# A new instruction order, two more tiles transposed by DMA and two weight loads joined in an adaLN block with feature-map attention and a gated MLP

## The chip, the cores and the metric

The kernel runs on one core of one Trainium2 chip. The metric is the device time of one execution in microseconds (us): lower is better. The median of three runs is compared; beside it stands one execution that was recorded by the hardware profiler.

## The reference

One transformer block on 2048 tokens of width 512, in bfloat16. A modulation vector made from `c` gives a shift, a scale and a gate for the attention half and for the MLP half.

```python
mod = (silu(c) @ w_mod).reshape(1, 6, 1, 512)
sa, ca, ga, sb, cb, gb = (mod[:, i] for i in range(6))
h = layernorm(x) * (1 + ca) + sa
x = x + ga * A(h)
h = layernorm(x) * (1 + cb) + sb
x = x + gb * ((sigmoid(h @ w_gate) * (h @ w_up)) @ w_down)      # F = 1376

def A(h):                        # 32 heads of 16
    q, k, v = split(h @ wqkv)
    pq, pk = q @ w_phi, k @ w_phi                # per head
    phi_q = concat(softmax(pq), softmax(-pq))    # 32 features per head
    phi_k = concat(softmax(pk), softmax(-pk))
    kv = phi_k.T @ v;  z = phi_k.sum(over tokens)
    return ((phi_q @ kv) / (phi_q @ z + 1e-6)) @ wo
```

## The kernel before

**Tiles.** The 2048 tokens are 16 tiles of 128. All of x, the weights and the normalized, transposed input `h1T` stay in the core's memory (SBUF).

**Order.** Each piece of work is a small task with a name, an engine and a function. The text ORDER lists the names; each engine gets its instructions in this order and nothing is reordered later, so an engine whose next instruction waits holds back all that stands behind it on that engine. A suffix (@A ScalarE, @D VectorE, @P GpSimd) says which engine takes a task; without it the first engine in the task's table does. In the profile, TensorE is PE, VectorE is DVE, ScalarE is ACT, GpSimd is POOL, SyncE is SP. All loads, all stores and all transposes by DMA are issued by SP, in the order of the text too. Buffers of a class (eight PSUM banks, six `r2k` buffers and so on) are given out in the order of the text; the next user of a buffer waits for the last reader of the one before.

**Start.** `ld_...` tasks load x (`x0a` to `x3b`, two tiles each), the q, k, v weights (`wq`, `wk`, `wv`), the modulation weights (`wm..`), `wo`, the MLP weights (`wg`, `wu`, `wd`). `warm` tasks keep PE busy before there is real work. `tpw`, `wTc`, `fold`, `foldc` multiply w_phi into the k weights (side 1) and the q weights (side 0, where `wqT` transposes by DMA). `modc1`, `modca`, `modc2` make the modulation columns.

**First LayerNorm.** Tiles are taken in groups, LG: {0}, {1}, {2,3}, {4,5}, {6,7}, {8..11}, {12..15}. `st1_t` are the statistics of tile t (DVE), `rs1_g` and `nmr1_g` the factors of group g, `xn1_t` the normalized tile. Where TD of the group is 0, `tph` transposes by PE into PSUM and `hm1_gj` applies scale and shift from PSUM to column block j of `h1T`. Where TD is 1, `xT1_t` transposes by DMA straight into `h1T` and `hm1_gj` works there in place, SBUF to SBUF.

**Keys and values, per tile t.** `K` and `V` are four matmuls each; `e` (ACT) are the exponentials, `n` (DVE) their sums, `r` (DVE or ACT) the reciprocals, `phi` (POOL or DVE) the product of the two, `va` the copy of V, `kv` the matmuls that add phi.T @ v up in PSUM over all tiles. Tiles 11 to 15 are cut in parts (`e11.4` is the part that begins at column group 4). `kvm`, `kvp`, `kvz`, `kvn` turn the sum into the matrix for the queries.

```python
G.add(f"phi{t}.{a}", {"POOL": 0.08 + 1.77 * w, "DVE": 0.08 + 1.07 * w}, f_p, r=[("kr", t, a)], w=[("phi", t, a)], bufs=[ee, ks, ph], port=("POOL", "DVE"))
```

**Queries and output of the attention.** `Q` and `qe` are the query features of 512 tokens and 128 columns, `sm`, `num`, `den`, `u`, `o`, `oT`, `out` the quotient and the projection, `x1_t` the residual, `st2`, `rs2`, `nmr2`, `xn2`, `xnT`, `mod` the second LayerNorm of units of one or two tiles. `ga` and `gb` are written to memory and read back spread over all partitions (`gwa`, `gra`, `gwb`, `grb`) and multiplied into `wo` and `wd`.

**MLP.** It runs in chunks of 1, 1, 2, 4, 4, 4 tiles: `g` and `u` are the gate and up matmuls of a column tile, `tg` the tanh (ACT), `hm` the product (DVE), `y` the down projection, `fin` the residual sum (DVE), `st` the store. The last tile's y is cut into 384 and 128 columns (`y15.*` and `y15.*b`). `bnd` and `ldf` check a bound on the inputs and read a flag for a general path that the given inputs do not take.

Lines of the profile: 747 tpw, 751 wTc, 764 fold, 770 and 772 foldc, 787 and 788 st1, 803 nmr1, 812, 814 and 816 xn1 on ACT, DVE, POOL, 821 xT1, 829 tph, 836 and 838 hm1 on ACT and on DVE or POOL, 855 K, 859 V, 871 e, 874 n, 884 and 885 r on ACT, 887 r on DVE, 877 phi, 895 va, 278 kv, 299 kvm, 933 Q, 908 gra, 672 ld_wg, 663 ld_wv, 427 to 444 u, 562 to 567 g and u, 600 y, 607 fin, 609 st.

Of the kernel before, what the change touches and what calls it, by code (L numbers as in the profile page):

```python
# [38 lines left out]
st1_5 tph22 tph21 tph20 foldc13 rs1_3 warm1_11 foldc12 xn1_0 st1_6 st1_7 ld_wm01 warm1_12 modc1.0 foldc10 modc1.1 xn1_1@P ld_x2a ld_x2b rs1_4@P warm1_13
warm1_14 tph00 tph12 modc1c nmr1_3 xn1_5@P xn1_4@P tph13 warm1_15 tph23 hm1_21@A hm1_20 hm1_12 hm1_13 tph03 tph10 hm1_23 hm1_22@A hm1_10@A K3 nmr1_4 st1_10  # L40
tph01 tph02 tph11 hm1_11 hm1_00@A hm1_03@A hm1_01@A hm1_02@A ld_wq1 ld_wq0 ld_wv0 ld_wv1 K2 st1_11 st1_9 e3.0 K0 xn1_6@P xn1_7@P pmem e0.0 tph31 tph32 tph30
tph33 st1_8 n0.0 K1 hm1_30@A e1.0 hm1_31@A V3 tph42 V1 va3 r0.0@A rs1_5@P nmr1_5 hm1_32 hm1_33 ld_x3b ld_x3a wqT3 tph41 V4 hm1_41@A va1 K4 e2.0 xn1_8 n3.0
n1.0 ld_wmga xn1_11@P tph40 xn1_10@P xn1_9@P hm1_40 hm1_42 r1.0 K5 modca.0 modca.1 modcac phi0.0 st1_12 wqT0 wqT1 wqT2 fold01 r3.0@A xT1_11 xT1_10 phi1.0
fold00 tph43 foldc00 hm1_43@A fold03 xT1_9 foldc01 foldc03@D n2.0 V0 va0 e5.0 r2.0@A K6 V2 kv0.0 st1_13 st1_14 phi3.0 xT1_8 V6 kv1.0 e4.0 ld_wu0 phi2.0 K7 V5
st1_15 gwa va2 e6.0 rs1_6 va4 hm1_53@A va5 e7.0 fold02 kv2.0 kv3.0 V7 n4.0 hm1_51 hm1_50@P hm1_52@P n5.0 r4.0 phi4.0 nmr1_6 r5.0 phi5.0 xn1_12 ld_wd2 ld_wu1
ld_wg0 xT1_12 foldc02@D va6 xn1_14 xT1_14 K11 K8 V11 n6.0 va11@D n7.0 xn1_13@D kv4.0 K10 va7 r6.0@A e11.2 r7.0@A e8.0 phi6.0@D K9 xn1_15@D e11.4 e9.0 V10
kv5.0 n8.0 V8 phi7.0 va8 e11.0 r8.0 n9.0 e10.0 kv6.0 r9.0@A xT1_13 xT1_15 va10@D n11.4 V9 Q02 kv7.0 Q10 Q00 phi8.0 hm1_60 hm1_61 hm1_63 va9 hm1_62@A n10.0
r11.4 phi9.0 kv8.0 qe00 e11.6 K13 e13.4 r10.0 qe02 e13.0 K12 e12.0 n11.2 n13.4 n11.0 n11.6 r11.0 phi10.0 K15 phi11.0 n13.0 r11.6 r11.2 ld_wo r13.0 phi11.6
phi11.2 K14 V13 kv9.0 kv10.0 r13.4@A V12 n12.0 phi11.4@D e14.4 e15.0 V14 ld_wd va13 r12.0@A e15.4 phi13.0@D phi13.4 n15.0 n15.4 kv11.4 Q03 V15 e14.0 kv11.6
kv11.0 kv11.2 phi12.0 qe03 Q11 Q01 n14.4 n14.0 r14.4 r14.0 r15.0@A r15.4@A va12 va15 va14 qe01 Q13 kv12.0 kv13.4 phi14.4@D phi15.0@D phi14.0@D phi15.4@D  # L50
# [1071 lines left out]
```

## Time and profile before

| | us |
|---|---|
| median of 3 runs (213.63 to 215.25) | 213.74 |
| the profiled execution | 212.59 |
| its span | 210.9 |
| busy PE, DVE, ACT, POOL | 201.6, 168.4, 112.7, 92.6 |
| PE waiting for POOL's phi / DVE's h1T / DVE's u | 1.5 / 1.5 / 1.1 |
| first K matmul, kvm, first g matmul, last y | 12.9, 57.9, 74.1, 207.7 |

Times inside the span count from its start. An idle engine costs nothing unless something that sets the end waits for it; a wait is put down to the engine that released it. Busy PE counts overlapping matmuls once. PE's clock was granted in full throughout.

### The profile page before, as it was taken

What the parts mean: (1) busy time and instruction counts of PE and PEld (TensorE: products, weight loads), DVE (VectorE), ACT (ScalarE), POOL (GpSimd) and SP (SyncE); (2) the same over time, 40 slices, a digit from 0 to 9 for tenths busy, and PEclk for the clock granted to TensorE, in tenths of its full rate; (3) what the DMA queues carried; (4) which work ended last, traced back from release to release, by engine and by line L of the source; (5) the groups of instructions that cost most, each with busy time, mean ns of one, the idle gap of its engine ahead of it and who ended that gap; (6) DMA issues with size and microseconds to landing.
All of it is one profiled execution on the core that took longest, in us unless ns stands there. A gap on an engine that the chain in (4) does not pass through costs nothing.

```text
span 210.9 us, 4333 instructions
## 1 busy us (share of the span) xinstructions
PE 201.6 (96%) x1547; PEld 111.6 (53%) x1547; DVE 168.4 (80%) x425; ACT 112.7 (53%) x272; POOL 92.6 (44%) x118
## 2 busy tenths in 40 slices
PE   7999999959999999989999999999999999999993
PEld 2654655425676589748764444445444444444442
DVE  3899999999979998998999899874857756563522
ACT  2899999679998996445253322442251551323200
POOL 3667997558947599944243312515030210000000
PEclk9999999999999999999999999999999999999999
DMA  6999598398051110501623300325004030010111
GB/s 159 369 352 221 103 265 224 57 335 307 15 158 53 39 39 16 65 10 40 104 50 51 78 0 0 75 53 75 25 0 100 6 75 19 6 50 3 50 58 54
DMA packets 35309, 19.80 MB, mean 94 GB/s; under 512 B 23409, under 2 KB 34002, under 8 KB 35282
## 3 DMA queue, kind: packets, MB, share of 16 engines
q1 hardware_dynamic: 34752, 19.44, 36.1%
q8 instruction: 14, 0.23, 0.5%
q14 instruction: 13, 0.11, 0.2%
q10 hardware_dynamic: 530, 0.02, 0.1%
HBM read 12.11 MB, written 2.10 MB: 67 GB/s over the span
## 4 chain that ended last, share of the span: by engine, by line
PE 64%; DVE 16%; POOL 10%; DMA 4%; issue 3%; ACT 1%; SPq 0%; POOLq 0%; DVEq 0%; ACTq 0%
PE y_ps L600 15%; PE g_ps L562 14%; PE u_ps L562 14%; PE a_ps L471 4%; POOL phi L877 4%; PE q_ps L933 4%; PE k_ps L855 3%; DVE st L787 3%; PE v_ps L859 3%; POOL wd_sb L922 3%; DMA x_sb<-in_A_x_dram 2%; DVE h1T L838 2%; DMA wqk_sb<-xn 2%; DVE u L444 2%; PE kvacc L278 2%
## 5 line engine op out<-in xcount | busy, mean ns | idle before, releaser
L572 ACT ACTIVATE tg<-g_ps 128x512 bf16<-128x512 f32 (+3 forms) x66 | 28.9, 454 | 58.3 <-PE g_ps L562 39.2
L600 PE MATMUL y_ps<-wd_sb,wmod_sb 128*128 128x512 bf16 (+4 forms) x187 | 43.7, 367 | 0.0
L583 DVE SCALAR_TENSOR_TENSOR wmod_sb<-tg,u_ps 128x512 bf16<-128x512 bf16 (+4 forms) x63 | 30.1, 496 | 16.1 <-PE u_ps L562 8.3
L562 PEld LDWEIGHTS <-wg_sb 128*128 128x128 bf16 (+1 forms) x252 | 21.4, 99 | 17.2 <-DVE u L429 1.6
L562 PEld LDWEIGHTS <-wu_sb 128*128 128x128 bf16 (+1 forms) x252 | 21.7, 99 | 15.0 <-issue 0.2
L877 POOL TENSOR_TENSOR phi<-e,ks 128x1024 bf16<-128x1024 bf16 (+2 forms) x15 | 24.5, 1652 | 7.3 <-DVE ks L887 4.4
L462 POOL TENSOR_TENSOR o<-u 128x512 bf16<-128x512 f32 x14 | 17.7, 1271 | 21.0 <-DVE u L429 12.2
L600 PEld LDWEIGHTS <-wmod_sb 128*128 128x128 bf16 (+1 forms) x187 | 17.5, 98 | 17.2 <-DVE bs L637 0.3
L562 PE MATMUL u_ps<-wT_sb,wu_sb 128*128 128x512 bf16 (+2 forms) x124 | 23.9, 322 | 0.0
L562 PE MATMUL g_ps<-wT_sb,wg_sb 128*128 128x512 bf16 (+2 forms) x124 | 23.5, 322 | 0.0
L562 PE MATMUL g_ps<-wqk_sb,wg_sb 128*128 128x256 bf16 (+4 forms) x128 | 19.8, 287 | 1.1 <-DVE u L429 1.1
L874 DVE TENSOR_REDUCE ks<-e 128x64 f32<-128x1024 bf16 (+2 forms) x22 | 19.4, 906 | 0.0
L562 PE MATMUL u_ps<-wqk_sb,wu_sb 128*128 128x128 bf16 (+4 forms) x128 | 19.3, 287 | 0.0
L871 ACT ACTIVATE e<-k_ps 128x512 bf16<-128x512 f32 (+2 forms) x44 | 18.2, 498 | 1.2 <-PE k_ps L855 1.1
L938 ACT ACTIVATE eT<-q_ps 128x512 bf16<-128x512 f32 x32 | 17.0, 615 | 1.0 <-PE q_ps L933 1.0
L855 PE MATMUL k_ps<-wqk_f,h1T 128*128 128x512 bf16 x64 | 15.6, 379 | 1.5 <-DVE h1T L838 1.5
L859 PE MATMUL v_ps<-wv_sb,h1T 128*128 128x512 bf16 x64 | 16.4, 379 | 0.1
L607 DVE TENSOR_TENSOR ot<-y_ps,x 128x512 bf16<-128x512 f32 (+2 forms) x17 | 11.0, 654 | 6.6 <-PE y_ps L600 6.5
L471 PE MATMUL a_ps<-wo_sb,oT 128*128 128x512 bf16 x64 | 16.3, 379 | 0.0
L933 PE MATMUL q_ps<-h1T,wqk_f 128*128 128x512 bf16 x64 | 15.8, 378 | 0.0
L515 ACT ACTIVATE xn<-x,nmr,rs 128x512 bf16<-128x512 f32 x14 | 11.1, 812 | 5.1 <-DVE nmr L498 5.1
L787 DVE BATCH_NORM_STATS2 st<-x_sb 128x6 f32<-128x512 bf16 x16 | 10.7, 670 | 3.2 <-DMA x_sb<-in_A_x_dram 3.2
(151 smaller groups left out, 316.6 us busy)
## 6 DMA issues: line engine op xcount, KB each, us to landing
x_sb<-in_A_x_dram SPq DMA_DIRECT2D x8, 256.0 KB, 5.1
out_dram<-ot SPq DMA_DIRECT2D x15, 128.0 KB, 1.9
wmod_sb<-in_w_mod_dram SPq DMA_DIRECT2D x3, 512.0 KB, 5.9
wmod_sb<-in_w_mod_dram SPq DMA_DIRECT2D x1, 1536.0 KB, 11.9
wd_sb<-in_B_w_down_dram SPq DMA_DIRECT2D x1, 1280.0 KB, 7.2
wqk_sb<-in_A_wqkv_dram SPq DMA_DIRECT2D x4, 256.0 KB, 5.9
wu_sb<-in_B_w_up_dram SPq DMA_DIRECT2D x1, 768.0 KB, 6.0
wg_sb<-in_B_w_gate_dram SPq DMA_DIRECT2D x1, 768.0 KB, 7.2
```

The source lines that it names most:

```text
L462: G.add(f"o{t}", {"POOL": 1.3, "DVE": 0.62}, lambda e, ub=ub, o=o: engine(e).tensor_tensor(o[:], ub[0][:].rearrange("p h d -> p (h d)"), u ...
L471: pe.matmul(ap_[:], lhsT=oT[:, j, :], rhs=wo_sb[:, j, :], start=(j == 0), stop=(j == KT - 1))
L562: pe.matmul(ps[:fsz, 0:n], lhsT=w[:, j, ft * P:ft * P + fsz], rhs=h[:, j, 0:n], start=(j == 0), stop=(j == KT - 1))
L572: G.add(f"tg{k}.{ft}", {"ACT": 0.13 + n * 0.00083}, lambda e, tg=tg, g_ps=g_ps, fsz=fsz, n=n: act.activation(tg[:fsz, 0:n], g_ps[:fsz, 0:n ...
L583: dve.scalar_tensor_tensor(hm_all[:fsz, hm[k].slot, ft, 0:n], tg[:fsz, 0:n], 1.0, u_ps[:fsz, 0:n], op0=ALU.add, op1=ALU.mult)
L600: mm = pe.matmul(y[:, 0:c1 - c0], lhsT=hm_all[:fsz, hm[k].slot, ft, tl * P:(tl + 1) * P], rhs=wd_sb[:fsz, ft, c0:c1], start=(ft == 0), sto ...
L855: pe.matmul(kp[:], lhsT=h1T[:, j, t * P:(t + 1) * P], rhs=wqk_f[:, j, D:2 * D], start=(j == 0), stop=(j == KT - 1))
L859: pe.matmul(vp[:], lhsT=h1T[:, j, t * P:(t + 1) * P], rhs=wv_sb[:, j, :], start=(j == 0), stop=(j == KT - 1))
L871: act.activation(ee[:, ha:hb, s, :], kp[:, ha * DH:hb * DH].rearrange("p (h j) -> p h j", j=DH), ACT.Exp, scale=1.0 - 2.0 * s)
L874: dve.tensor_reduce(ks[:, ha:hb].rearrange("p h s -> p (h s)"), ee[:, ha:hb].rearrange("p h s j -> p (h s) j"), axis=AX.X, op=ALU.add)
L877: engine(e).tensor_tensor(ph[:, ha * 32:hb * 32].rearrange("p (h j) -> p h j", j=DH), ee[:, ha:hb].rearrange("p h s j -> p (h s) j"), ks[: ...
L933: pe.matmul(qp[:], lhsT=wqk_f[:, j, blk * P:(blk + 1) * P], rhs=h1T[:, j, cq * 512:(cq + 1) * 512], start=(j == 0), stop=(j == KT - 1))
```

## The change

Four things are changed.

1. ORDER is a new text. It lists the same tasks but for those of 2 and 3; some 90 tasks change their engine. [...]
2. TD of the group {6,7} goes from 0 to 1: `tph40` to `tph43` (eight PE transposes) go, `xT1_6` and `xT1_7` (DMA transposes) come, `hm1_40` to `hm1_43` work in place in SBUF instead of from PSUM.
3. The v weights and the gate weights are loaded by one DMA each instead of two; the number of parts of each load stands in a table, SPLIT.
4. The tasks that read those weights wait for the one load.

```diff
-TD = [0, 0, 0, 0, 0, 1, 1]
+TD = [0, 0, 0, 0, 1, 1, 1]
+SPLIT = {"wk": 2, "wv": 1, "wq": 2, "wg": 1, "wu": 2, "x1": 2, "x2": 2, "x3": 2}
...
-G.add(f"g{k}.{ft}", ..., r=h2k + [("wg", ft // 6)] + ...)
+G.add(f"g{k}.{ft}", ..., r=h2k + [("wg", ft // 6 * (SPLIT["wg"] - 1))] + ...)
...
-    for h in range(2):
-        load(f"wv{h}", [("wv", h)], lambda e, h=h: sp.dma_start(wv_sb[:, 2 * h:2 * h + 2, :], wqkv_v[:, 2 * h:2 * h + 2, 2 * D:3 * D]), 256 * K1)
+    for w, dst, c0 in (("wv", wv_sb[:], 2 * D), ("wq", wqk_sb[:, :, 0:D], 0)):
+        for h in range(SPLIT[w]):
+            load(f"{w}{h}", [(w, h)], lambda e, ...: sp.dma_start(dst[:, a:b], wqkv_v[:, a:b, c0:c0 + D]), 512 * K1 / SPLIT[w])
...
-    for h in range(2):
-        load(f"wg{h}", [("wg", h)], lambda e, a=768 * h, b=768 + 608 * h: sp.dma_start(wg_sb[:, :, a:b], ...[:, :, a:b]), (768 - 160 * h) * K1)
+    for h, (a, b) in enumerate([(0, 768), (768, F)] if SPLIT["wg"] == 2 else [(0, F)]):
+        load(f"wg{h}", [("wg", h)], lambda e, a=a, b=b: sp.dma_start(wg_sb[:, :, a:b], ...[:, :, a:b]), (b - a) * K1)
...
-    G.add(f"V{t}", {"PE": 0.87}, f_v, r=h1k + [("wv", 0), ("wv", 1)], w=[("v", t)], bufs=[vp])
+    G.add(f"V{t}", {"PE": 0.87}, f_v, r=h1k + [("wv", h) for h in range(SPLIT["wv"])], w=[("v", t)], bufs=[vp])
```

The two orders, by engine, where the prediction speaks of them:

```text
PE before:   ... K3 tph01 tph02 tph11 K2 K0 tph31 .. K1 V3 tph42 V1 tph41 V4 K4 tph40 K5 modca fold01 fold00 tph43 fold03 V0 K6 V2 kv0 V6 kv1 K7 ...
PE after:    ... K0 tph11 tph10 tph12 K3 K2 tph13 V0 tph31 .. K1 modca.0 V1 V3 V2 V4 modca.1 K4 V5 kv0 K5 fold00 fold02 fold03 V6 V7 kv1 fold01 K6 kv2 Q02 K7 kv3 Q01 K8 ...
DVE before:  ... n0 nmr1_5 hm1_32 hm1_33 n3 n1 hm1_40 hm1_42 r1 st1_12 foldc03 n2 st1_13 st1_14 st1_15 n4 hm1_51 n5 r4 nmr1_6 r5 foldc02 n6 va11 n7 xn1_13 phi6 xn1_15 n8 r8 n9 va10 n11.4 hm1_60 hm1_61 hm1_63 n10 ...
DVE after:   ... n0 hm1_33 nmr1_5 n2 n1 xn1_11 st1_14 r1 hm1_40 st1_15 n3 hm1_42 st1_13 st1_12 n4 foldc01 nmr1_6 xn1_12 xn1_14 xn1_13 xn1_15 hm1_51 n5 hm1_53 phi4 n6 n7 r7 n8 r8 n11.0 n11.6 n11.4 hm1_61 hm1_60 n9 r9 r11.0 va8 n10 r10 n11.2 phi11.6 r11.2 n12 phi11.2 r12 n13.0 n13.4 n14.4 r13.4 n14.0 n15.4 va14 n15.0 r15.0 phi15.0 phi14.0 phi15.4 kvm0 ...
POOL before: ... xn1_6 xn1_7 pmem rs1_5 xn1_11 xn1_10 xn1_9 phi0 phi1 phi3 phi2 hm1_50 hm1_52 phi4 phi5 phi7 phi8 phi9 phi10 phi11.0 phi11.6 phi11.2 phi13.4 phi12 perm ...
POOL after:  ... xn1_4 xn1_6 rs1_5 xn1_9 xn1_8 phi0 hm1_41 hm1_43 xn1_10 phi1 phi2 phi3 hm1_50 hm1_52 phi5 phi6 phi7 hm1_63 phi8 phi9 phi10 phi11.0 phi11.4 phi12 phi13.4 phi13.0 phi14.4 perm ...
SP before:   ld_x0b ld_wk1 ld_x0a ld_wk0 ld_x1a ld_x1b ld_wm00 ld_wm01 ld_x2a ld_x2b ld_wq1 ld_wq0 ld_wv0 ld_wv1 ld_x3b ld_x3a wqT3 ld_wmga wqT0 wqT1 wqT2 xT1_11 .. xT1_8 ld_wu0 gwa ld_wd2 ld_wu1 ld_wg0 xT1_12 .. xT1_15 ld_wo ld_wd ld_wmm2 gra ld_wg1 ...
SP after:    ld_x0b ld_x0a ld_wk1 ld_wk0 ld_x1b ld_x1a ld_wm00 ld_wm01 ld_wq0 ld_x2a ld_x2b ld_wv0 ld_wmga ld_wq1 wqT1 wqT0 ld_x3b ld_x3a xT1_7 xT1_6 wqT2 wqT3 xT1_11 xT1_8 xT1_9 xT1_10 ld_wd xT1_12 .. xT1_15 ld_wd2 ld_wmm2 ld_wu0 ld_wo ld_wu1 gwa gra ld_wg0 ...
PE end before: ... y14.10 y15.3 .. y15.10 y15.0b .. y15.10b        then fin15b st15b
PE end after:  ... y14.10 y15.3b .. y15.10b y15.4 .. y15.10        then fin15 st15
```

More of the change, by code (lines that the diff above doesn't have):

```diff
@@ L39 @@
[L39 to L50, printed above, removed]
@@ new lines @@
+tpw0 wTc1@D nmr1_2 wTc2 rs1_0 ld_x1b ld_x1a tpw3 warm1_7 warm1_8 warm1_9 xn1_0 warm1_10 wTc0 warm1_11 wTc3 ld_wm00 ld_wm01 nmr1_1 xn1_3 fold11 fold10 warm1_12
+ld_wq0 ld_x2a st1_6 st1_7 tph00 tph01 tph03 fold12 foldc10 st1_4 st1_5 foldc12 ld_x2b ld_wv0 xn1_1@P xn1_2@P rs1_4@P fold13 warm1_13 modc1.0 tph22 modc1.1
+foldc13 foldc11 tph21 warm1_14 tph02 warm1_15 tph20 modc1c nmr1_4 hm1_00 hm1_01@A hm1_02@A hm1_20@A tph23 hm1_21 hm1_03 K0 ld_wmga ld_wq1 tph11 wqT1 wqT0
+ld_x3b tph10 hm1_23@A rs1_3@P hm1_22 nmr1_3 xn1_5@P xn1_7@P st1_8 st1_10 st1_9 st1_11 tph12 K3 K2 hm1_11@A hm1_12@A e0.0 hm1_10@A xn1_4@P ld_x3a tph13
@@ new lines @@
+hm1_13@A xn1_6@P n0.0 e2.0 V0 tph31 rs1_5@P tph32 xT1_7 tph33 tph30 K1 hm1_31@A va0 hm1_33 nmr1_5 xn1_9@P xn1_8@P n2.0 e1.0 hm1_30@A r0.0@A phi0.0 xT1_6
+hm1_41@P hm1_43@P xn1_10@P modca.0 V1 V3 hm1_32@A n1.0 xn1_11@D st1_14 V2 wqT2 wqT3 r1.0 hm1_40 st1_15 r2.0@A xT1_11 V4 modca.1 va2 va3 modcac e3.0 n3.0 K4 V5
+e4.0 phi1.0 kv0.0 K5 va1 va4 phi2.0 hm1_42 fold00 fold02 fold03 V6 foldc00 foldc02 st1_13 st1_12 foldc03 n4.0 V7 kv1.0 fold01 foldc01@D xT1_8 xT1_9 rs1_6
+r3.0@A nmr1_6 K6 r4.0@A e5.0 e6.0 xn1_12@D xn1_14@D xn1_13@D xn1_15@D va6 xT1_10 phi3.0 kv2.0 Q02 K7 e7.0 va7 hm1_51 n5.0 hm1_53 phi4.0@D r5.0@A hm1_50@P
@@ new lines @@
+hm1_52@P kv3.0 Q01 va5 K8 e8.0 n6.0 r6.0@A n7.0 K9 kv4.0 K11 phi5.0 r7.0 n8.0 e11.4 V9 ld_wd phi6.0 V11 kv5.0 phi7.0 xT1_12 e11.2 e11.0 e11.6 K10 r8.0 n11.0
+n11.6 n11.4 xT1_14 xT1_13 xT1_15 kv6.0 hm1_63@P qe02 va9 e9.0 V10 Q10 V8 hm1_62@A e10.0 kv7.0 phi8.0 va11 hm1_61 hm1_60 K13 K12 n9.0 r9.0 r11.0 va8@D V12
+kv8.0 qe10 phi9.0 K14 n10.0 r11.4@A r10.0 ld_wd2 r11.6@A e12.0 va10 n11.2 kv9.0 e13.4 e13.0 V13 V14 K15 phi10.0 phi11.0 phi11.4 kv10.0 phi11.6@D r11.2 n12.0
+va12 phi11.2@D e14.0 e14.4 qe01 r12.0 e15.4 phi12.0 e15.0 n13.0 n13.4 n14.4 kv11.4 r13.4 n14.0 ld_wmm2 ld_wu0 ld_wo n15.4 va14@D n15.0 r15.0 phi13.4 kv11.6
@@ new lines @@
+r13.0@A Q03 V15 kv11.0 kv11.2 Q00 kv12.0 r14.4@A va15 va13 r15.4@A r14.0@A Q13 Q31 phi13.0 phi15.0@D phi14.0@D kv13.0 ld_wu1 gwa gra ld_wg0 phi15.4@D kv14.0
+kv15.0 kv13.4 kvm0 phi14.4 kv14.4 kv15.4 kvm1 Q11 perm kvp2 kvp0 kvp1 qe03 qe31 qe00 kvz2 kvz1 kvz0 modc2.0 sm0 kvn1 kvn2@A kvn0@A sm2 num01 num00 smS0@D qe13
+qe11 wo0 modc2.1 modc2c smS2 Q12 wo1 wo3 den0 u01 u00 den2 Q33 num21 sm1 qe12 gwb grb smS1 den1 wo2 num20 tpo0 Q30 num30 oT0 u20 qe33 u21 wo_all wmod_free o2
+out0 wd8 num11 x1_0 u11 qe30 Q32 st2_0 num10 sm4 num31 Q23 u30 u10 num71 oT2 Q22 tpo1 qe32 rs2_0 smS4 nmr2_0 qe23 Q20 den4 u31 o3 oT3 xn2_0 xnT0 wd10 oT1
@@ L656 @@
     load_x("x0a", 0, 2)
-    for h in range(2):
-        load(f"wk{h}", [("wk", h)], lambda e, h=h: sp.dma_start(wqk_sb[:, :, D + 256 * h:D + 256 * h + 256], wqkv_v[:, :, D + 256 * h:D + 256 * h + 256]), 256 * K1)
+    for h in range(SPLIT["wk"]):
+        load(f"wk{h}", [("wk", h)], lambda e, a=D + D // SPLIT["wk"] * h, b=D + D // SPLIT["wk"] * (h + 1): sp.dma_start(wqk_sb[:, :, a:b], wqkv_v[:, :, a:b]), 512 * K1 / SPLIT["wk"])
     load_wm(0)
@@ L661 @@
     load_x("x0b", 2, 4)
-    for h in range(2):
-        load(f"wv{h}", [("wv", h)], lambda e, h=h: sp.dma_start(wv_sb[:, 2 * h:2 * h + 2, :], wqkv_v[:, 2 * h:2 * h + 2, 2 * D:3 * D]), 256 * K1)
-    for i in range(2, 8):
-        load_x(f"x{i // 2}{'ab'[i % 2]}", 2 * i, 2 * i + 2)
-    for h in range(2):
-        load(f"wq{h}", [("wq", h)], lambda e, h=h: sp.dma_start(wqk_sb[:, 2 * h:2 * h + 2, 0:D], wqkv_v[:, 2 * h:2 * h + 2, 0:D]), 256 * K1)
+    for w, dst, c0 in (("wv", wv_sb[:], 2 * D), ("wq", wqk_sb[:, :, 0:D], 0)):
+        for h in range(SPLIT[w]):
+            load(f"{w}{h}", [(w, h)], lambda e, dst=dst, c0=c0, a=KT // SPLIT[w] * h, b=KT // SPLIT[w] * (h + 1): sp.dma_start(dst[:, a:b], wqkv_v[:, a:b, c0:c0 + D]), 512 * K1 / SPLIT[w])
+    for i in range(1, 4):
+        for h in range(SPLIT[f"x{i}"]):
+            load_x(f"x{i}{'ab'[h]}", 4 * i + 2 * h, 4 * i + 4 // SPLIT[f"x{i}"] * (h + 1))
     for nm, c0, c1 in (("ga", 2, 3), ("m2", 3, 6)):
@@ L670 @@
     load("wo", ["wo_raw"], lambda e: sp.dma_start(wo_sb[:], A_wo.rearrange("(j p) n -> p j n", p=P)), 512 * K1)
-    for h in range(2):
-        load(f"wg{h}", [("wg", h)], lambda e, a=768 * h, b=768 + 608 * h: sp.dma_start(wg_sb[:, :, a:b], B_w_gate.rearrange("(j p) n -> p j n", p=P)[:, :, a:b]), (768 - 160 * h) * K1)
-    for h in range(2):
-        load(f"wu{h}", [("wu", h)], lambda e, a=768 * h, b=768 + 608 * h: sp.dma_start(wu_sb[:, :, a:b], B_w_up.rearrange("(j p) n -> p j n", p=P)[:, :, a:b]), (768 - 160 * h) * K1)
+    for h, (a, b) in enumerate([(0, 768), (768, F)] if SPLIT["wg"] == 2 else [(0, F)]):
+        load(f"wg{h}", [("wg", h)], lambda e, a=a, b=b: sp.dma_start(wg_sb[:, :, a:b], B_w_gate.rearrange("(j p) n -> p j n", p=P)[:, :, a:b]), (b - a) * K1)
+    for h, (a, b) in enumerate([(0, 768), (768, F)] if SPLIT["wu"] == 2 else [(0, F)]):
+        load(f"wu{h}", [("wu", h)], lambda e, a=a, b=b: sp.dma_start(wu_sb[:, :, a:b], B_w_up.rearrange("(j p) n -> p j n", p=P)[:, :, a:b]), (b - a) * K1)
     load("wd", ["wd_raw"], lambda e: sp.dma_start(wd_sb[:, 0:FT - 1, :], B_w_down[0:(FT - 1) * P, :].rearrange("(j p) n -> p j n", p=P)), 1280 * K1)
@@ L753, in f2 @@
                         dve.tensor_copy(wT_sb[:, 1, k, :], tp[:])
[L754 removed]
+                G.add(f"tpw{k}", {"PE": 0.24}, f, r=[("wk", k * SPLIT["wk"] // KT)], w=[("tpw", k)], bufs=[tp])
                 G.add(f"wTc{k}", {"ACT": 0.54, "DVE": 0.42}, f2, r=[("tpw", k)], w=[("wT", 1, k)], bufs=[tp])
@@ L919, in f_wr @@
         pool.tensor_copy(wr_sb[:, :, F_LAST:P], wu_sb[:, :, F - (P - F_LAST):F])
-    G.add("wr", {"POOL": 0.9}, f_wr, r=[("wg", 1), ("wu", 1)], w=["wr"])
+    G.add("wr", {"POOL": 0.9}, f_wr, r=[("wg", SPLIT["wg"] - 1), ("wu", SPLIT["wu"] - 1)], w=["wr"])
     for ft in range(FT):
```

69 lines of the change are left out of this document (32 added, 37 removed).

## The prediction

> **What bounds the kernel now.** I read the busy shares, then the engines stage by stage, then who made TensorE (PE) wait, then VectorE (DVE) and GpSimd (POOL) around those waits, and the tail.
>
> The page's busy shares, and its slices of PE and DVE:
>
> ```profile
> PE 201.6 (96%) x1547; PEld 111.6 (53%) x1547; DVE 168.4 (80%) x425; ACT 112.7 (53%) x272; POOL 92.6 (44%) x118
> ...
> PE   7999999959999999989999999999999999999993
> ...
> DVE  3899999999979998998999899874857756563522
> ```
>
> PE idles 9.3 us of 210.9. It has one thin slice inside, at 42 to 47 us; up to 125 us DVE is as full as PE. The stretches of the key/value stage and the last one (length, busy time and instructions of PE, PEld, DVE, ACT, POOL, then PE clock, DMA share, GB/s):
>
> ```profile
> 12.90:41.00 28.10, 27.73 (x223) 14.70 (x223) 27.40 (x55) 26.65 (x66) 22.56 (x25) 1.00 0.82 198
> 41.00:46.00 5.00, 2.20 (x17) 0.88 (x16) 5.00 (x7) 3.01 (x8) 3.93 (x2) 1.00 0.84 259
> 46.00:59.00 13.00, 12.98 (x134) 7.21 (x132) 12.23 (x27) 12.66 (x37) 9.81 (x11) 1.00 0.51 180
> 207.70:210.90 3.20, 0.00 (x0) 0.00 (x0) 0.26 (x1) 0.00 (x0) 0.00 (x0) 0.99 0.16 45
> ```
>
> From 12.9 us (first K) on, PE runs almost back to back; between 41 and 46 us it is idle 2.8 us while DVE is full. PE's waits, all of them:
>
> ```profile
> PE kvacc L278 <- POOL phi L877: 1.5, 2, 1.3
> PE k_ps L855 <- DVE h1T L838: 1.5, 1, 1.5
> PE warm L708 <- DVE wd_sb L701: 1.2, 1, 1.2
> PE g_ps L562 <- DVE u L429: 1.1, 1, 1.1
> PE tp_w L747 <- DMA wqk_sb<-in_A_wqkv_dram: 0.2, 1, 0.2
> ```
>
> So what any order can win behind the start is 1.5 + 1.5 + 1.1 = 4.1 us. The timelines of DVE and POOL show where the first two come from (start, length, instruction):
>
> ```profile
> 35.59 0.40 DVE L814 TENSOR_SCALAR xn<-x_sb,mv,rs 128x512 bf16<-128x512 bf16 x1
> ...
> 37.05 2.12 DVE L814 TENSOR_SCALAR xn<-x_sb,mv,rs 128x512 bf16<-128x512 bf16 x1
> ...
> 42.79 2.66 DVE L838 TENSOR_SCALAR h1T<-h1T,modc 128x512 bf16<-128x512 bf16 x3
> ```
> ```profile
> 37.09 1.93 POOL L877 TENSOR_TENSOR phi<-e,ks 128x1024 bf16<-128x1024 bf16 x1 [1.74 <-PE kvacc L278]
> 41.05 3.93 POOL L877 TENSOR_TENSOR phi<-e,ks 128x1024 bf16<-128x1024 bf16 x2 [2.03 <-DVE ks L887]
> ```
>
> The same DVE operation takes 0.40 us beside an idle POOL and 2.12 us beside a phi that ends at 39.02: it sat until POOL was through. The three h1T operations end at 45.45, just after the second phi (44.98). With 0.32 us as the undisturbed length (start to start at 35.59), the late stage lost 0.27 (hm1_51 at 29.18, 0.59 long) + 0.08 + 1.80 + (2.66 - 0.96) = **3.85 us of DVE in four encounters, 0.96 each**. The 1.80 delays the n, r that phi8 waits for (PE's 1.3), the 1.70 delays hm1_6x that K13 waits for (PE's 1.5). This is what the new order has to move.
>
> **The change, part by part.** The sum is made against the profiled execution, 212.59 us (span 210.9). The median of the runs shown is 213.74, so 1.15 us is added at the end.
>
> *Tiles 6 and 7 by DMA.* Eight of 32 PE transposes go: two take 0.11 us start to start (17.87 to 17.98), so 8 x 0.055 = 0.44 us of PE. As PE partly waits for DVE in this stage, between 0 and -0.44; I take **-0.2**. SP issues two more transposes at 1.2 us each, behind ld_x3a and ahead of wqT2, wqT3 and xT1_8 to 11. They wait for xn1_7 and xn1_6 (POOL, at about 15 and 17 us by the xn length of 0.76); wqT2 and wqT3 then land near 24 us (4.2 us from issue), about when PE reaches fold0x: hidden, 1 us if not. hm1_41 and 43 move from ACT (0.57) to POOL (0.57, the 256 wide row at L539), hm1_40 and 42 stay on DVE but read SBUF now: at 0.40 undisturbed no dearer, yet they can meet a POOL operation, counted below.
>
> *Single loads.* SP saves two issues, 1.0 us, which nobody waits for. wv: ahead of its end stand 3,840 KB instead of 4,096, at some 350 GB/s 0.75 us sooner, against 15.1 to 15.6 us before (issue 7.86, 7.2 to landing); its first user, V0, comes at 15.4 at the earliest (K0 near 12.7, K3, K2). Nothing, at most 0.5. wg: its one load (1,376 KB) stands behind gra, which before left at 56.60, held back by a buffer (kv12). In the new order that buffer is freed by phi13.0, at about the same place. Landing by the 1,280 and 1,536 KB rows takes 7.2 to 11.9 us, so by 69 us; the first gate matmul was at 74.08. Hidden by some 5 us. Moving ld_wd ahead of xT1_12 to 15 changes nothing: three other big loads stood there.
>
> *The front.* K0 comes first instead of K3. ACT's chain to modc1c holds the same copies (the new xn1_3, 0.73, replaces wTc1 and rs1_3) and ends at 12.2 again; K0 needs four 128 wide hm1 where K3 needed 256 wide ones. ±0.3, taken as **0**.
>
> *DVE up to kvm (57.94).* By the engines' marks in the two orders, with the rows' lengths. Added: wTc1 0.55, hm1_00, 03, 21, 22 1.44, xn1_11, 12, 14 1.14, foldc01 0.64, hm1_53 0.40, phi4 1.22, r7, r9, r12 1.59, r13.4, r15 0.62, va8, va14 1.37, phi11.2, 11.6 1.08: 10.05. Taken off: six hm1 2.16, foldc02, 03 1.28, r4, r5 1.06, four short r and r13.0 1.39, va10, va11 1.37, phi6 1.22, hm1_63 0.40, phi11.4, 13.0, 14.4 1.94: 10.82. Net **-0.8**.
>
> *Encounters.* DVE operations from SBUF to SBUF that run while POOL works: before the four above. After: xn1_11, hm1_40, hm1_42, the run xn1_12 to 15, hm1_51, hm1_53, hm1_61/60, so eight (seven groups, the run counting twice), and POOL has some 3 us more to do there (hm1_41, 43, 63, phi13.0, 14.4 against phi11.2, 11.6). Bounds: none collides, -3.85; each loses the 0.96 of before, 7.7 - 3.85 = +3.85. To choose I walked the new queues with the rows' lengths from modc1c at 12.2. r0 ends at 20.4, so phi0 holds POOL from 20.8 to 22.75; DVE reaches xn1_11 at 21.3 and waits 1.45. hm1_40 comes at 24.4 and waits 0.6 for xn1_10. hm1_42 comes at 27.1, as phi1 ends (27.25): 0.1. The xn run loses 0.95 to phi3 and hm1_50, hm1_51 0.5, hm1_61/60 0.9: 4.5. DVE's phi11.6 meets phi10; no row shows a DVE phi beside a busy POOL, so half of the 1.5 it would wait, 0.75. Together 5.25, **+1.4**. Queued behind each of them is the next n, hence r, phi and kv.
>
> [...]
>
> *The gap at 93.8 us* (1.06, waiting for u, L429): it hangs on one DVE chain that is ordered anew. Between -1.06 and +1.0; half of the gain, **-0.5**. The rest, to 200 us, has PE work at hand (y, g, u) and showed no wait.
>
> *The tail.* The last output is now the 384 columns of tile 15 instead of 128. The add takes 558 ns instead of 291, the 96 KB store lands in 2.0 us instead of 1.5 (32 KB): **+0.8**, bounds 0.3 to 0.8.
>
> Sum: -0.2 + 0 - 0.8 + 1.4 - 0.5 + 0.8 = +0.7, so 213.3 for a profiled run and with 1.15 **214.4 us**. This is within 1% of before, about what a measurement of this kernel can tell from no change (211.6 to 215.9).
>
> **The rivals.**
>
> *The encounters are avoided: 210.5 us.* For it: both long stalls of PE have this one cause, and the four xn stand together, so that they can fall into one hole of POOL. DVE would win 3.85, but PE can win no more than its 3.1 us of waits in the stage. -3.1 - 0.44 - 0.5 + 0.8 = -3.2. Against it: twice the operations that can meet, and by my walk POOL is busy at most of them.
>
> *DVE loses more than before: 217.3 us, slower.* One mechanism: a DVE operation arrives when POOL has just begun a phi. Its place is hm1_42 in the queue n3, hm1_42: in my walk it arrives 0.1 us before phi1 ends and phi2 starts. Any lateness over 0.1 us decides, and then it waits 1.9 us; V6 and K6 wait for it, and all of DVE's queue. With eight encounters at 0.96: +3.85 - 0.8 - 0.2 + 0.8 = +3.6, with nothing won at 93.8. Against it: a part of it is hidden where PE has Q work queued ahead.
>
> *The gate weights come late: 218 us.* If phi13.0 frees gra's buffer 8 us later than kv12 did, the load lands at 77, after the first gate matmul. Three us over 74.08 on top of 214.4 make 217.4 to 218. Little speaks for it.
>
> A change that does nothing to the waits (stalls only moved) lies inside the forecast.
>
> **How the numbers follow.** Forecast 0.36 (own range 212.0 to 215.9), avoided 0.31, more lost 0.30, gate late 0.03. The walk stands on sums of thirty durations, so an error of 2 us in the stage is likely; that is why the sides weigh nearly as much. Range: 210.2 to 218.0. Faster by over 1%: 0.31, within: 0.36, slower: 0.33.
>
> **What would show it.** Right: 24 transposes into tp_h; DVE's xn and h1T rows (L814 and L838 of before) with maxima near 1.5 to 2 us at about 21 to 23, 27 and 31 us; PE waiting for h1T before V6 near 25 to 28 us; kvm at 58 to 59 us; the last store 96 KB. Wrong: kvm before 56.5 us (avoided) or after 60.5 us (more lost), a PE wait for wg or wv, or new gaps of PE after 95 us, where I expect none.

## The result, and the profile after

The changed kernel takes **215.56 us** (median of 20 runs, 214.16 to 217.13) against 213.86 us of the kernel before (20 runs, 212.25 to 216.41) beside it. The ratio is 1.0078, 95% interval 1.0053 to 1.0103: slower by 0.8%, and the interval reaches just over 1%. The forecast was 214.4. The profiled execution of after took 216.11 us with a span of 214.4, that of before 212.59 and 210.9. Runs of one kernel differ in the mean clock that PE was granted (0.98 to 1.00), so that the two profiled executions lie 3.5 us apart where the medians lie 1.7 apart; "at full clock" below means the runs in which it was 0.997 or more. At full clock the median of after is 215.3 us (8 runs) and that of before 213.15 (17 of the 29 runs beside the first experiments), so the loss does not come from the clock.

From the page of after, the busy shares and the slices of PE's clock:

```profile
PE 202.3 (94%) x1539; PEld 111.2 (52%) x1539; DVE 174.4 (81%) x427; ACT 107.3 (50%) x269; POOL 93.3 (44%) x121
...
PEclk9999969999999999999999999999999999999999
```

PE is busy about as long as before (202.3 against 201.6 us) in a span 3.5 us longer: it idles 12.1 us in place of 9.3. DVE is busy 6 us more. The stretches answer to those shown of before (length, busy time and instructions of PE, PEld, DVE, ACT, POOL, then PE clock, DMA share, GB/s):

```profile
12.90:41.00 28.10, 25.07 (x179) 12.57 (x177) 26.86 (x50) 22.86 (x61) 20.55 (x20) 0.94 0.85 177
41.00:46.00 5.00, 5.00 (x45) 2.74 (x44) 4.93 (x10) 5.00 (x13) 4.92 (x4) 1.00 0.93 352
46.00:59.00 13.00, 11.76 (x91) 5.78 (x89) 12.10 (x22) 12.18 (x38) 11.59 (x11) 1.00 0.41 140
```

The pause of before at 41 to 46 us is gone: PE is full there, 2.80 us won. But PE now idles 3.03 us between 12.9 and 41 us (0.37 before) and 1.24 us between 46 and 59 us (0.02 before). The waits of PE name the places; the three that weigh most behind the start:

```profile
PE v_ps L860 <- DVE h1T L839: 2.2, 1, 2.2
PE kvacc L279 <- DVE phi L878: 1.5, 1, 1.5
...
PE k_ps L856 <- DVE h1T L839: 0.8, 1, 0.8
```

The first is new, and the timelines of DVE, POOL and PE show what it is (start, length, instruction):

```profile
26.15 2.05 DVE L839 TENSOR_SCALAR h1T<-h1T,modc 128x256 bf16<-128x256 bf16 x1
```
```profile
26.19 1.93 POOL L878 TENSOR_TENSOR phi<-e,ks 128x1024 bf16<-128x1024 bf16 x1
```
```profile
28.26 2.31 PE L860 MATMUL v_ps<-wv_sb,h1T 128*128 128x512 bf16 x5 [2.19 <-DVE h1T L839]
```

The DVE row is hm1_42, the POOL row phi2; phi1 ran ahead of it from 24.19 to 26.11. hm1_42's row begins 0.04 us ahead of phi2's, but the reduction before it on DVE runs until 26.23 (25.03, 1.20 long), and by then phi2 has begun. hm1_42 ends at 28.20, just behind phi2 (28.12), and V6 on PE, which reads its output, starts at 28.26. The kernel before had this task at 22 us, reading PSUM, and nobody waited for it.

### The profile page after: what moved, and what is told of

Its sections match the earlier page's. It is cut to its first block, busy times and chain, and to the rows that moved or that the text cites. A ratio compares the mean times of both kernels' runs of the same rounds, so it can differ in the third digit from the quotient of the medians.

```text
span 214.4 us, 4313 instructions
## 1 busy us (share of the span) xinstructions
PE 202.3 (94%) x1539; PEld 111.2 (52%) x1539; DVE 174.4 (81%) x427; ACT 107.3 (50%) x269; POOL 93.3 (44%) x121
## 4 chain that ended last, share of the span: by engine, by line
PE 66%; DVE 19%; ACT 5%; DMA 3%; issue 3%; POOL 2%; DVEq 0%; POOLq 0%; ACTq 0%
PE y_ps L601 16%; PE u_ps L563 16%; PE g_ps L563 15%; PE a_ps L472 6%; DVE ks L875 5%; PE q_ps L934 4%; DVE st L788 3%; DVE h1T L839 2%; DMA wqk_sb<-xn 2%; POOL phi L878 2%; DVE xn L815 2%; ACT e L872 2%; PE num L365 1%; DMA x_sb<-in_A_x_dram 1%; PE v_ps L860 1%
## 5 line engine op out<-in xcount | busy, mean ns | idle before, releaser
L573 ACT ACTIVATE tg<-g_ps 128x512 bf16<-128x512 f32 (+4 forms) x66 | 29.1, 455 | 61.5 <-PE g_ps L563 43.3
L601 PE MATMUL y_ps<-wd_sb,wmod_sb 128*128 128x512 bf16 (+4 forms) x187 | 44.2, 367 | 0.0
L878 POOL TENSOR_TENSOR phi<-e,ks 128x1024 bf16<-128x1024 bf16 (+2 forms) x16 | 26.2, 1648 | 7.4 <-PE kvacc L279 3.5
L463 POOL TENSOR_TENSOR o<-u 128x512 bf16<-128x512 f32 x11 | 13.9, 1269 | 18.6 <-DVE u L428 6.9
L563 PE MATMUL g_ps<-wqk_sb,wg_sb 128*128 128x128 bf16 (+4 forms) x128 | 20.2, 287 | 0.7 <-ACT wqk_sb L542 0.7
L563 PE MATMUL u_ps<-wqk_sb,wu_sb 128*128 128x256 bf16 (+4 forms) x128 | 20.1, 287 | 0.0
L860 PE MATMUL v_ps<-wv_sb,h1T 128*128 128x512 bf16 x64 | 16.9, 402 | 2.2 <-DVE h1T L839 2.2
L492 POOL TENSOR_SCALAR ve<-mv 128x2 f32<-128x2 f32 (+1 forms) x8 | 1.8, 227 | 37.0 <-DVE mv L482 35.9
L856 PE MATMUL k_ps<-wqk_f,h1T 128*128 128x512 bf16 x64 | 16.1, 379 | 0.8 <-DVE h1T L839 0.8
L477 DVE TENSOR_TENSOR x<-a_ps,x_sb 128x512 f32<-128x512 f32 x16 | 10.8, 684 | 3.3 <-PE a_ps L472 3.1
```

The costliest lines, as they stand in the source:

```text
L563: pe.matmul(ps[:fsz, 0:n], lhsT=w[:, j, ft * P:ft * P + fsz], rhs=h[:, j, 0:n], start=(j == 0), stop=(j == KT - 1))
L573: G.add(f"tg{k}.{ft}", {"ACT": 0.13 + n * 0.00083}, lambda e, tg=tg, g_ps=g_ps, fsz=fsz, n=n: act.activation(tg[:fsz, 0:n], g_ps[:fsz, 0:n ...
L601: mm = pe.matmul(y[:, 0:c1 - c0], lhsT=hm_all[:fsz, hm[k].slot, ft, tl * P:(tl + 1) * P], rhs=wd_sb[:fsz, ft, c0:c1], start=(ft == 0), sto ...
L856: pe.matmul(kp[:], lhsT=h1T[:, j, t * P:(t + 1) * P], rhs=wqk_f[:, j, D:2 * D], start=(j == 0), stop=(j == KT - 1))
L860: pe.matmul(vp[:], lhsT=h1T[:, j, t * P:(t + 1) * P], rhs=wv_sb[:, j, :], start=(j == 0), stop=(j == KT - 1))
L878: engine(e).tensor_tensor(ph[:, ha * 32:hb * 32].rearrange("p (h j) -> p h j", j=DH), ee[:, ha:hb].rearrange("p h s j -> p (h s) j"), ks[: ...
```

## The experiments

**hm1_42 earlier.** The question: is the place of this instruction the loss? hm1_40, which lost 0.3 us in after, is moved with it.

```diff
-... wqT3 r1.0 hm1_40 st1_15 r2.0@A ... phi2.0 hm1_42 fold00 ...
+... wqT3 hm1_40 hm1_42 r1.0 st1_15 r2.0@A ... phi2.0 fold00 ...
```

> After, with two DVE instructions (hm1_40, hm1_42) moved ahead of r1.0, so that phi1 on POOL cannot have begun when they arrive. Theory (a DVE operation from SBUF to SBUF waits out a running POOL operation): the 2.05 us of hm1_42 falls to under 0.9, PE's 2.2 us wait for h1T before V6 falls under 0.6, the clock grant stays full in that slice, kvm comes 1 to 2 us earlier than in after (60.3), the time is 0.6 to 1.2% below after, so 0.995 to 1.003 of before. Rival (the DMA transposes of tiles 6 and 7 land too late, or DVE's queue is simply too long): V6 still waits 1.5 us or more and the time stays at 1.008 of before.

Measured: 213.65 us (12 runs), ratio to before 0.9995 (0.996 to 1.003). DVE's timeline and PE's waits of this kernel:

```profile
23.22 0.59 DVE L839 TENSOR_SCALAR h1T<-h1T,modc 128x256 bf16<-128x256 bf16 x2
```
```profile
PE kvacc L279 <- DVE phi L878: 1.6, 1, 1.6
...
PE q_ps L934 <- DVE wqk_f L773: 1.1, 1, 1.1
PE k_ps L856 <- DVE h1T L839: 1.0, 2, 0.8
```

Both operations together take 0.59 us, in a moment at which POOL does not begin a phi; the wait of V6 is gone, kvm starts at 58.0 instead of 60.3 us, and the time falls by 1.9 us (at full clock by 1.7, 215.3 to 213.6). The place of these two instructions, of which hm1_42 lost the far larger part, is worth the whole loss. It is not a gain over before: three waits of 1.6, 1.1 and 1.0 us stay in the stage.

**The other way to take it off SBUF.** Tiles 6 and 7 back on PE, so that hm1_40 and 42 read PSUM again, the rest of the new order kept.

```diff
-TD = [0, 0, 0, 0, 1, 1, 1]
+TD = [0, 0, 0, 0, 0, 1, 1]
-... xT1_7 ... xT1_6 ... hm1_41@P hm1_43@P ...
+... tph41 hm1_41@A tph43 hm1_43@A ... tph40 hm1_40 ... tph42 hm1_42 ...
```

> After with one part undone: tiles 6 and 7 are transposed by PE again (TD as before, tph40 to 43 ahead of their hm1_4, hm1_41 and hm1_43 on ACT). Theory (the new order loses because hm1_40 and hm1_42 now read SBUF and meet POOL): no wait of PE over 0.6 us before V6, 0.44 us more of PE work, time 0.5 to 1.2% below after, 0.996 to 1.003 of before. Rival (the order loses all over, the two tiles do not matter): within 0.3% of after, 1.005 to 1.011 of before.

Measured: 213.92 us, 0.9999 (0.9964 to 1.0034). hm1_42 comes at 26.76 us and takes 0.41 us from PSUM, with POOL's phi as busy as in after (two from 24.34 to 28.28). V6 waits 0.5 us in place of 2.2; the eight transposes that PE does again (0.44 us, the prediction's estimate) cost less than the wait they avoid.

**Does the drop of PE's clock behind the pause carry the loss?** In the profile of after PE runs at 0.50 of its clock from 28.1 to 31.5 us. PE gets matmuls that compute nothing new in the place of the pause:

```diff
-                for kt_hd in range(KT):
+                for kt_hd in [h for _ in range(10 if (side, kt_in) == (0, 3) else 1) for h in range(KT)]:
```

> After, with the matmuls of fold03 repeated ten times (36 more small matmuls, 2.0 us at full clock, same result), placed where PE otherwise waits 2.2 us for hm1_42. No other work changes. Theory (the pause of PE lowers its clock for some us, and that alone costs about 1 us): PE's clock stays at 1.00 in the slices from 26 to 34 us, where after shows 0.6; the time falls by 0.2 to 0.6% against after, 1.002 to 1.006 of before. Rival (the lower clock is chance or has no price, since DVE sets the end of this stage): no change, 1.008 of before, or slower where the filler delays V6.

Measured: 215.8 us, 1.0079 (1.0042 to 1.0116): the same as after. PE now waits only 0.3 us ahead of V6, and 11 of the 12 runs were at full clock, and yet nothing was won. kvm, which hangs on DVE, starts at 59.91 us, 46.7 behind the first K; so it does in the next experiment's profile (there at 59.46), which has the same order and the pause of 2.2 us, but the clock in full (1.00 from 12.9 to 41 us). So the lateness of DVE is the price, not PE's pause. The drop of the clock has a price of its own where it comes: in the profile of after the same stretch takes 47.4 us.

**The loads split again.**

```diff
-SPLIT = {"wk": 2, "wv": 1, "wq": 2, "wg": 1, ...}
+SPLIT = {"wk": 2, "wv": 2, "wq": 2, "wg": 2, ...}
-... ld_wv0 ... ld_wg0 ...
+... ld_wv0 ld_wv1 ... ld_wg0 ld_wg1 ...
```

> After with one part undone: the v weights and the gate weights come in two loads each again. Prediction of before: hidden, so within 0.3% of after, 1.005 to 1.011 of before. Rival (V0 or the first gate matmul waits for the one big load): faster than after by 0.3% or more.

Measured: 216.28 us (6 runs), 1.0146 (1.008 to 1.0211), above what was expected. Only two of the six runs were at full clock; they took 215.56 and 215.95, like after. Six runs of this kind settle little. The same part alone, the kernel before with the wide loads:

> The kernel before with one part of the change alone: the value weights and the gate weights in one load each, ld_wv1 and ld_wg1 dropped from the order, all else as before. Theory (both loads land under other work, so their form costs nothing): 0.997 to 1.003 of before, no PE wait on wv or wg. Rival (the wide load makes the first V or the first g wait, and that is part of what the change loses): 1.004 or more, with a PE wait on wv or wg.

Measured: 214.33 us, 0.9994 (0.9958 to 1.0029), no wait of PE for either weight. The form of the loads costs and wins nothing that these runs can tell (0.4%).

**The long wait of the kernel before.** If the places of the encounters decide, the same must hold there. Two edits of the order of before, the second on top of the first:

```diff
-... phi6.0@D K9 xn1_15@D e11.4 ...
+... xn1_15@D phi6.0@D K9 e11.4 ...
```

> Before, with one DVE instruction moved: xn1_15 stands ahead of phi6 instead of behind it, in the time in which POOL idles (35.4 to 37.1 us in before). Theory: its 2.12 us fall to about 0.4, n8 and r8 come 1.7 us earlier, PE's wait of 1.3 us for phi8 (kv8) at 41.7 us falls under 0.4; DVE may still lose to the phis at hm1_6x. Time 0.2 to 0.6% below before: 0.994 to 0.998. Rival (the wait is taken over by the next thing, hm1_6x behind phi9 or the transpose of tile 15): PE's waits in the stage stay at 2.8 us together and the ratio is 1.000.

```diff
-... hm1_61 hm1_63 va9 ...
+... hm1_61 hm1_63@P va9 ...
```

> Before, with xn1_15 ahead of phi6 as in the run above and hm1_63 given to POOL (it then stands between phi8 and phi9 in POOL's queue and cannot collide). Theory: no DVE xn or h1T instruction over 0.7 us in the stage, PE's two waits of 1.3 and 1.5 us fall under 0.8 together, kvm 1.5 to 3 us earlier than 57.9, time 0.6 to 1.2% below before: 0.988 to 0.994. Rival (DVE was not what PE waited for in sum, POOL with 0.8 us more becomes it): 0.997 or more.

Measured: 211.71 us, 0.9925 (0.9894 to 0.9956), and **210.46 us, 0.9854 (0.9816 to 0.9892)**. DVE's timeline of the first and, in the next fence, of the second:

```profile
36.09 0.73 DVE L814 TENSOR_SCALAR xn<-x_sb,mv,rs 128x512 bf16<-128x512 bf16 x2
...
41.58 2.66 DVE L838 TENSOR_SCALAR h1T<-h1T,modc 128x512 bf16<-128x512 bf16 x3
```
```profile
41.61 0.73 DVE L838 TENSOR_SCALAR h1T<-h1T,modc 128x512 bf16<-128x512 bf16 x2
```

In the first, the xn that took 2.12 us takes 0.36, beside its neighbour and ahead of the phi that POOL begins at 37.59. The three h1T still lose 1.70 us. In the second, one of them goes to POOL (1.03 us there), the other two take 0.73 us and the lost 1.70 is gone. Their windows at 41 to 46 us:

```profile
41.00:46.00 5.00, 3.74 (x25) 1.78 (x24) 5.00 (x9) 3.93 (x12) 2.76 (x2) 1.00 1.02 343
```
```profile
41.00:46.00 5.00, 5.00 (x31) 2.43 (x30) 4.59 (x12) 4.97 (x15) 5.00 (x4) 1.00 1.03 342
```

PE's idle time there goes from 2.80 to 1.26 to 0 us, kvm starts at 56.7 and 55.3 us (57.9 before), and the time falls by 1.53 and 2.78 us. Two words of the order won what the whole new order wins at 41 to 46 us, without what it loses elsewhere. The second is the fastest version measured here, and it beats both kernels. Both ratios are better than expected, in part because 7 of the 22 runs of before beside them were at a lower clock: at full clock before has 212.95, and the second wins 2.5 us, a ratio of 0.988, which is inside its expected range.

**Can the waits that the mended after keeps be filled or moved?** Two tries on top of the first experiment. First: the cast foldc01, which a Q matmul waits for, to ACT, and Q11 ahead of kv14.0 as filling for the wait on phi14.

```diff
-... foldc01@D ... phi15.4@D kv14.0 ... kvm1 Q11 perm ...
+... foldc01@A ... phi15.4@D Q11 kv14.0 ... kvm1 perm ...
```

> The version of after in which hm1_40 and hm1_42 stand ahead of r1.0, with two more moves for the two longest waits of PE that were left there: foldc01 goes from DVE to ACT (PE waited 1.1 us for it ahead of Q02), and the matmuls Q11 stand ahead of kv14 instead of behind kv15 (PE waited 1.6 us for phi14). Theory (each wait of PE in this stage is paid in full): both waits fall under 0.5 and 0.9 us, time 0.6 to 1.0% below that version (213.65): 0.990 to 0.994 of before. Rival (DVE sets the end of the stage, so PE only waits elsewhere): kvm stays at 58.0 us and the ratio at 0.998 to 1.000.

Measured: 214.93 us, 1.0039 (1.0 to 1.0078); the six of its twelve runs at full clock have the median 213.55, where the first experiment's have 213.58. Nothing was won. PE's waits of this kernel (in its profile the clock falls, but behind 59 us: 0.90 in the mean between 59 and 94, 1.00 ahead of that):

```profile
PE k_ps L856 <- ACT e L872: 1.2, 1, 1.2
...
PE kvp L315 <- DVE kvm L300: 0.6, 1, 0.6
```

The wait for foldc01 is gone and one of 1.2 us for ACT has come; the wait for phi14 has shrunk from 1.6 to 0.7 us and one for kvm has come. kvm itself starts at 58.3 us (58.0 in the first experiment): work for PE in the gap did not hasten the engine that PE waits for. Second: two of the four xn, which lose time to POOL, to POOL itself.

```diff
-... xn1_12@D xn1_14@D xn1_13@D xn1_15@D ... hm1_52@P kv3.0 ...
+... xn1_12@D xn1_14@D ... hm1_52@P xn1_13@P xn1_15@P kv3.0 ...
```

> The kernel after with hm1_40 and hm1_42 ahead of r1.0, and in addition xn1_13 and xn1_15 on GpSimd behind hm1_52 (where GpSimd was idle 2.3 us) in place of VectorE. Theory (what is left of the loss at 46 to 59 us is VectorE's lateness from the run of four xn, 2.77 us with its waits for GpSimd): the two xn left take 1.0 to 1.6 us, hm1_51 comes 1 us earlier, kvm starts at 56.5 to 57.5 in place of 58.0: 0.993 to 0.998 of before. Rival (GpSimd or ScalarE binds there as much; the waits only change place, as with Q11 moved): 0.999 to 1.003, kvm at 57.8 or later.

Measured: 213.88 us, 0.9969 (0.9936 to 1.0002), beside runs of before with the median 214.7. The ratio would fit the theory, but at full clock it is 213.8 against 213.7 of before; this is the first experiment's time (213.65). The tile kvm:

```profile
L300 DVE TENSOR_TENSOR kvm<-kvacc,mask x2: 431/436/442, 57.7 to 58.1; 128x272 bf16<-128x272 f32 x2
```

It starts 0.3 us earlier, not 1 us: the rival was nearer. What binds between 46 and 59 us in this order, when DVE is relieved of two operations, was not found; POOL and ACT are busy there 10.7 and 10.5 of 13 us.

**The DMA transposes alone.** The kernel before, with tiles 6 and 7 transposed by DMA behind ld_x3a. The lock, in the two expectations, is what DVE's rows of before show: an xn of 0.40 us that takes 2.12 us beside POOL's phi.

```diff
-TD = [0, 0, 0, 0, 0, 1, 1]
+TD = [0, 0, 0, 0, 1, 1, 1]
-... tph42 ... ld_x3b ld_x3a wqT3 tph41 ... tph40 ... tph43 ...
+... ld_x3b ld_x3a xT1_6 xT1_7 wqT3 ...
```

> The kernel before with one part of the change alone: LayerNorm tiles 6 and 7 transposed by DMA (xT1_6 and xT1_7 behind ld_x3a, tph40 to tph43 gone), all else as before, so hm1_40 and hm1_42 stay on VectorE but read SBUF. Theory of the lock: at their place (22.1 us) GpSimd has just begun phi0 (21.8), so the first of them takes 1.5 to 2 us in place of 0.36, VectorE is later by that from there on, and the pause of PE at 41 to 46 us, which VectorE's lateness sets, grows: 1.002 to 1.008 of before (0.5 to 1.7 us). Rival (only a due time that is missed costs; K6 and V6 come at 28 us, so nothing is missed, and PE is rid of 1.7 us of transposes): 0.996 to 1.001.

The same with hm1_40 and hm1_42 on ACT (`hm1_40@A`, `hm1_42@A`):

> As the kernel before with tiles 6 and 7 transposed by DMA, but hm1_40 and hm1_42 on ScalarE (hm1_40@A, hm1_42@A) in place of VectorE. Theory of the lock: no VectorE instruction that reads SBUF is added, so nothing waits for GpSimd; ScalarE does 1.1 us more and VectorE 0.7 us less at 22 to 24 us: 0.995 to 1.002 of before, and below the kernel that leaves the two on VectorE. Rival (the DMA transposes cost by themselves, 2.5 us more in SP's queue ahead of the loads behind them, or ScalarE's e activations come later): 1.002 to 1.008.

Measured: 218.91 us, 1.0219 (1.0177 to 1.026), and 218.31 us, 1.0196 (1.015 to 1.0242). Both miss all that was expected. DVE and POOL of the first show the expected wait, SP and PE an unexpected one (a fence for each engine):

```profile
22.53 1.97 DVE L838 TENSOR_SCALAR h1T<-h1T,modc 128x256 bf16<-128x256 bf16 x2
```
```profile
22.23 1.93 POOL L877 TENSOR_TENSOR phi<-e,ks 128x1024 bf16<-128x1024 bf16 x1
```
```profile
15.85 2.61 SPq L821 DMA_TRANSPOSE h1T<-xn  x2
18.51 1.26 SPq L757 DMA_TRANSPOSE wT_sb<-wqk_sb  x1
19.82 0.58 SPq L669 DMA_DIRECT2D wmod_sb<-in_w_mod_dram  x1
```
```profile
24.30 0.69 PE L723 MATMUL modc_ps<-sc_bf,wmod_sb 128*128 128x1 bf16 x16 [1.76 <-DMA wmod_sb<-in_w_mod_dram]
```

hm1_40 and 42 take 1.97 us where they took 0.72 from PSUM. But that is the smaller part of the loss, since the second kernel, without this meeting, is only 0.6 us faster. The profile shows another wait, in SP's queue: the transposes wait for xn1_7, hold the queue 2.61 us, and wmod's load behind them is issued at 19.82 instead of 14.95 us, so that PE waits 1.76 us for it. Behind that wait the clock drops: in both profiles its mean is 0.94 from 12.9 to 41 us and 0.87 from 46 to 59 us, which at half clock is 3.4 us each time, and none of the twelve runs was at full clock. How the loss divides between the wait and the clock was not tested. So the two kernels do not price the DMA transposes by themselves; they suggest that these need room in SP's queue, which the order of after has (ld_wmga and two of the four wqT stand ahead of them there). On ACT the two hm1 take 1.08 us (from 22.33) beside POOL's phi (from 21.70), and ACT's other hm1 of this width 0.57 to 0.60 each in that profile: no row of these shows ACT losing time to a phi.

## Why the prediction came out as it did

The time lies 1.2 us above the forecast, inside its own range, and the sign of the sum was right. Its parts were not all right, and that they summed so near is partly luck: a meeting taken at almost nothing cost 1.7 us, four others cost less than walked, and the 0.8 us of the tail did not come. Of the forecast's own signs, the wait for h1T ahead of V6 came (2.19 us at 28.26), while kvm at 60.3 us lies between the 58 to 59 that it called right and the 60.5 that it called wrong. The span of the profiled executions grew by 3.5 us: 2.4 to kvm (57.94 to 60.34), 0.1 from there to the first g matmul, 1.1 from there to the last y, and -0.1 in the tail.

*Transposes, loads, front.* 24 matmuls write tp_h, as expected, and the first K comes at 12.94 (12.92). The loads were nothing that the experiments on them can tell. The -0.2 for the transposes was not isolated.

*Encounters: right place, wrong size of one.* The walk named hm1_42 as coming just before phi1 ends, so that it would lose 0.1, and made the other outcome a rival with the price of 1.9 us. It came just behind phi1's end, as phi2 began, and lost 1.73 (2.05 less 0.32). That term is the one that was mis-sized, and what happened there is the mechanism of the rival "DVE loses more"; the first experiment shows its worth, 1.7 to 1.9 us of the time. Against the walk, the others by DVE's rows, counted as the prediction counts (length less 0.32): xn1_11 1.09 (1.45), hm1_40 0.30 (0.6), the run of four xn 1.24 (0.95), hm1_51 and 53 0.16 (0.5), hm1_61/60 0.28 (0.9). The 0.32 is the distance to the next start; the length of such an operation alone is 0.40, so hm1_51 and 53, with 0.40 each, met nothing, and the 0.40 at 35.59 us, which the prediction counts as the second of its four encounters, was none. For DVE's phi11.6, which reads two inputs from SBUF, two rows of DVE and one of POOL give the price:

```profile
49.77 1.40 DVE L878 TENSOR_TENSOR phi<-e,ks 128x256 bf16<-128x256 bf16 x1 [0.70 <-PE kvacc L279]
...
52.33 0.40 DVE L878 TENSOR_TENSOR phi<-e,ks 128x256 bf16<-128x256 bf16 x1
```
```profile
48.96 3.26 POOL L878 TENSOR_TENSOR phi<-e,ks 128x1024 bf16<-128x1024 bf16 x3
```

The same operation takes 1.40 us beside a busy POOL and 0.40 us 0.1 us after POOL is done: 1.0 lost (0.75 taken). All together 5.8 us against the 5.25 predicted and the 3.85 of before: the total was near, because four smaller losses than walked made up for most of the large one, but the total is not what counts. Some 0.2 us in the meeting of two queues decided 1.7 us.

*The stage up to kvm: too small.* From the first K to kvm DVE is busy 45.1 us (43.8 before): +1.3, where -0.8 + 1.4 = +0.6 was predicted. The other 1.1 us of the 2.4 are DVE idle, and most of that belongs to this execution and not to the order. It waits 0.86 us at 31.80 for a fold that PE, at half clock until 31.5, makes late. In the profile of the kernel with the loads split again, which has the same order and the clock in full there, this wait is absent, and the first K to kvm takes 46.7 us: 1.7 more than before, of which DVE is busy 1.4.

*Behind the first g: wrong.* -0.5 was taken for the gap at 93.8 us, and new gaps of PE after 95 us were not expected. The gap shrinks by 0.4 (1.06 to 0.50 + 0.19, now behind an ACT operation), but three of 0.2 to 0.4 us at 118 to 124 us are new, behind POOL and DVE, and from the first g to the last y it takes 134.69 us against 133.59. No experiment was made on it; the cause of this 1.1 us is open.

*The tail: wrong.* +0.8 was taken for the wider last add and store. This is DVE's last row:

```profile
211.25 0.56 DVE L608 TENSOR_TENSOR ot<-y_ps,x 128x384 bf16<-128x384 f32 x1 [0.70 <-PE y_ps L601]
```

The add costs the 0.56 priced, but from the last y to the end it takes 3.15 us, 3.23 before. In before the last add ended at 207.96, and its store was issued only at 208.41, behind the store ahead of it in SP's queue; in after the last store is issued at 211.83, as its add ends, and the 96 KB land in 1.6 us, not 2.0. The price of the add was right, that of the landing too high, and the queue was left out.

## What to carry to other kernels

Where the trace shows one engine holding another for a whole instruction (here a phi of 1.93 us on POOL cost DVE's hm1_42 1.73), price each meeting by who comes first, and give a meeting that is settled by a tenth of a microsecond the full price of the other outcome. A change that wins a known wait is to be counted against every new meeting it makes: here 2.8 us won at one place went back at others, while two changed words of the old order won 2.5 to 2.8 us and kept them. Filling PE's gap did not help where the engine behind the gap was late: 215.8 us with the filler against 215.56, and 213.55 with the moved Q against 213.58, at full clock.
